# Two transformer layers on one core: VectorE's share of the softmax exponentials, with a cubic or a quadratic polynomial

## The chip, the cores and the metric

The kernel runs on one core of a Trainium2 chip. The metric is the device time of one execution in microseconds, the median of the runs shown. The engines named below are TensorE (PE in the profile, with PEld for its weight loads), VectorE (DVE), ScalarE (ACT), GpSimd (POOL) and SyncE (SP, which issues the DMAs). Each runs its own instructions in program order and waits for the others through semaphores.

## What is computed

Two rounds of attention and a squared-ReLU MLP over 2,048 tokens of width 448, with 16 heads of width 28. All inputs are bf16.

```python
def _A_ref(x, wqkv, wo):
    B, S, D = x.shape
    H = 16; Dh = D // H
    qkv = (lambda x, *d: x.transpose(*d))((x @ wqkv).reshape(B, S, 3, H, Dh), 2, 0, 3, 1, 4)
    q, k, v = qkv[0], qkv[1], qkv[2]
    scale = Dh ** -0.5
    scores = jnp.einsum("bhqd,bhkd->bhqk", q, k) * scale
    p = _softmax(scores, axis=-1)
    o = jnp.einsum("bhqk,bhkd->bhqd", p, v)
    return (lambda x, *d: x.transpose(*d))(o, 0, 2, 1, 3).reshape(B, S, D) @ wo
def _B_ref(x, w1, b1, w2, b2):
    h = jnp.einsum("bsd,df->bsf", x, w1) + b1
    zero = jnp.zeros_like(h)
    r = jnp.where(h > zero, h, zero)
    h = r * r
    out = jnp.einsum("bsf,fd->bsd", h, w2) + b2
    return out
x = A_x
x = x + _A_ref(_layernorm(x, axis=-1), A_wqkv, A_wo)
x = x + _B_ref(_layernorm(x, axis=-1), B_w1, B_b1, B_w2, B_b2)
x = x + _A_ref(_layernorm(x, axis=-1), A_wqkv, A_wo)
x = x + _B_ref(_layernorm(x, axis=-1), B_w1, B_b1, B_w2, B_b2)
```

For each of the two layers, each of the 16 heads has 2,048 x 2,048 scores, and each score needs one exponential. No maximum is subtracted; the sum of the exponentials comes out of the product with V, which carries a column of ones.

## The kernel before

**Score banks.** The scores are cut into units of 128 keys by 512 columns, one PSUM bank each: four heads of a group are done side by side on TensorE (32 rows of the array each), with 256 queries and two key tiles in a unit (128 queries and four key tiles in the last two blocks of layer 1). There are 2,048 such units, or banks. `s_stream` (L818) writes them three at a time into a tile `sc` of three banks (L882); two such tiles alternate (`R_sc`).

**Who takes the exponential.** `e_stream` (L898) has ScalarE turn a whole `sc` tile into a bf16 tile `pt` with one ACTIVATE of Exp (L907), three banks wide, or two banks wide when VectorE takes the third. VectorE's way is `a_unit` and `a_rest` (L954 to L1008). The score arrives scaled by log2(e) times 2^17, so that after adding a bias and limiting it from below (`take`, L965, which writes an int32), the upper 16 bits count half octaves and the lower 16 bits are the place within the half octave. `power` (L981) builds a float of 2 to the half octave from the upper bits; `first` (L988) multiplies it by (f + root), where f is the lower half; `square` (L993) forms (f + lin) * f; `close` (L1003) adds `low` and multiplies with the result of `first`, and writes bf16 into a buffer `pd`. That is five VectorE instructions for a bank. They work in one of two sets of scratch buffers (`R_v`): the tiles v_i, v_e and v_h, or a part of `K_sb` that is not in use at the time. In the second set the result of `square` overwrites the score.

**Who decides.** The kernel text does not fix the order of the work. A planner (`Planner`, L143) runs while the program is built: it holds a clock for each engine, an estimated duration for each piece of work (the second argument of `Op`), and streams with priorities, and it always issues next the piece that can start first by its clocks. `apart` (L774) is asked at each `sc` tile whether VectorE takes the third bank. It says no, among other things, when the scratch sets are taken, when VectorE was occupied over a limit in the last 8 us of the planner's clock (`BUSY`, L797), or when the work that VectorE still owes, `left[0]`, passes `TB` or `TB2` (L799). `left[0]` grows by 2.74 for each bank taken (L970), and falls as its instructions are issued. So the number of banks that go to VectorE is a result of the planner, and durations written in the `Op`s change the order of everything.

**What else the engines do.** TensorE multiplies the exponentials with V (`p_stream`, L1065), and fills in between with projections, w_o, w1 and w2 (`mm_tile`, L606). VectorE empties those banks, does layer norms, the normalisation and the MLP's squared ReLU (L1261, L1268). When the planner sees TensorE little occupied, it repeats score matmuls (`again`, L875) or inserts matmuls whose result nobody reads (`heat`, L1319). While scores are left, ScalarE does nothing but Exp; after the last one (`s_left` empty) it also takes ReLUs and squares (`engs_now`, L440). The last two 128-token blocks of layer 1 go through w_o, layer norm and MLP in the tail (`chain`, L1204).

Of the kernel before, what the change touches and what calls it, by code (L numbers as in the profile page):

```python
# [11 lines left out]
DT = mybir.dt  # L12
AF = mybir.ActivationFunctionType
ALU = mybir.AluOpType
# [9 lines left out]


FRAC = 17
EXP_BIAS = -0.19498194355419685 * 2.0 ** FRAC
EXP_LOW = -56.0 * 2.0 ** FRAC
EXP_BASE = 72.0 * 2.0 ** 23 + 13573.0 * 2.0 ** 7
EXP_POLY = (4.12317870205982 * 2.0 ** 16, 3.06764719893404 * 2.0 ** 16, 29.439149859494734 * 2.0 ** 32)  # L30
OVER = 0.08
QUICK = 2
QUICK3 = 2
# [203 lines left out]
def kernel(  # L237
# [12 lines left out]
    nc = tc.nc  # L250
# [35 lines left out]
    R_v = (Res(1), Res(1))  # L286
# [477 lines left out]
    left = [0.0]  # L764

    def sets_of(unit):

        pi, kb, r, hh = unit
        l, qb, *_ = passes[pi]
        if l == 0:  # L770
            return R_v if 2 <= qb <= 6 else R_v[:1]
        return R_v
# [45 lines left out]
    def s_stream():  # L818
        while at[0] < len(units):
# [5 lines left out]
            def fn(e, gi=gi, us=us, js=js):  # L825
# [17 lines left out]
                if j is None:  # L843
                    next_at(js[-1] + 1)
                else:
                    if not own:
                        us, ks = us[:2], ks[:2]
                        gbuf[gi]["n"] = 2
                    us, ks = us + [units[j]], ks + [3]
                    taken.add(j)  # L850
                    held[0] += 1
                    pending[0] += 1
                    next_at(at[0])
                    if own:
                        x = gbuf[gi]["x"] = Op("PE", 0.0, None)
                        x.res = min((r for r in R_m if r.when() is not None), key=lambda r: r.when())
                        x.turn = len(x.res.rel)
                        x.res.rel.append(None)
                        dst.append(bank(x, "mt"))
                    else:  # L860
                        x = gbuf[gi]["x"] = o
                        o.need = 2
                    pl.spawn(C_PRIO, a_unit(gi, x, dst[-1], us[-1], passes[us[0][0]][0]))
# [28 lines left out]
    def apart_from(gi, t):  # L892

        if "read" in gbuf[gi]:
            tc.declare_no_dep(t.ins, gbuf[gi]["read"].ins, reason="both read the scores, in banks of their own")
        gbuf[gi]["read"] = t
# [21 lines left out]
    def pd_free(unit):  # L918

        pi, kb, r, hh = unit  # L920
        l, qb, *_ = passes[pi]
        if l == 0:
            return (R_pd[0], *(R_pd[1:5] if qb <= 6 else R_pd[3:5]))
        if len(norm_done.get((0, len(blocks[0]) - 1), ())) < G:
            return tuple(R_pd[:1])
        return tuple(R_pd[:1] + R_pd[6:]) if hidden_left[0] else tuple(R_pd[:1] + R_pd[5:])

    def pd_of(o):
        i = R_pd.index(o.res)
        if i == 0:  # L930
            return vp.tile([P, 512], DT.bfloat16, name="pd")[:, :]
        if i < 5:
            return V_sb[1][:, 11 + i, :, :].rearrange("p h r -> p (h r)")
        if i > 5:
            return V_sb[0][:, 8 + i, :, :].rearrange("p h r -> p (h r)")
        return hp.tile([P, QB], DT.bfloat16, name="h")[:, :]
# [5 lines left out]
    def set_of(res, l):  # L942

        k = R_v.index(res)
        two = lambda a: a.rearrange("p (a n) -> p a n", a=2)
        if k == 0:
            i, e, h = two(v_i[:, :]), two(v_e[:, :]), two(v_h[:, :])
        else:
            keys = K_sb[1 - l][:, :, S - 512:S] if l == 0 else K_sb[0][:, :, 0:512]
            i, e = keys[:, 0:2, :].bitcast(DT.int32), keys[:, 2:4, :].bitcast(DT.int32)  # L950
            h = i.bitcast(DT.float32)
        return i, e, h, two

    def a_unit(gi, x, src, unit, l):  # L954
        yield Op("-", 0.0, None, deps=[("s", gi)])
        box = {}

        def take(e):
            pending[0] -= 1
            box["i"], box["e"], box["h"], two = set_of(c.res, l)  # L960
            box["two"] = two
            halves = box["i"].bitcast(DT.uint16).rearrange("p a (n t) -> p a n t", t=2)
            box["f"] = halves[:, :, :, 0]
            box["n"] = box["i"].bitcast(DT.int16).rearrange("p a (n t) -> p a n t", t=2)[:, :, :, 1]
            t = nc.vector.tensor_scalar(out=box["i"], in0=two(src), scalar1=EXP_BIAS,  # L965
                                        scalar2=EXP_LOW, op0=ALU.add, op1=ALU.max)
            if x is gbuf[gi]["s"]:
                apart_from(gi, t)
        c = Op("DVE", 0.69, take, deps=[("s", gi)], acq=sets_of(unit), rel=x)
        left[0] += 2.74  # L970
        yield c
        left[0] -= 0.6
        pl.spawn(lambda now: V_LAST if e_now[1] - gi >= V_AGE or at[0] > ends_at[unit[0]] + V_PAST else V_LATE if now > c.end + V_WAIT else V_PRIO if gi > FIRST else V_FIRST, a_rest(gi, c, box, unit))

    def a_rest(gi, c, box, unit):

        root, lin, low = EXP_POLY
        flt = lambda k: box[k].bitcast(DT.float32)

        def power(e):  # L980
            nc.vector.tensor_scalar(out=box["e"], in0=box["n"], scalar1=2.0 ** 22, scalar2=EXP_BASE,  # L981
                                    op0=ALU.mult, op1=ALU.add)
        p = Op("DVE", 0.42, power, deps=[c])
        yield p
        left[0] -= 0.34

        def first(e):
            nc.vector.scalar_tensor_tensor(out=flt("e"), in0=box["f"], scalar=root, in1=flt("e"),  # L988
                                           op0=ALU.add, op1=ALU.mult)
        g = Op("DVE", 0.684, first, deps=[p])  # L990

        def square(e):
            nc.vector.scalar_tensor_tensor(out=box["h"], in0=box["f"], scalar=lin, in1=box["f"],  # L993
                                           op0=ALU.add, op1=ALU.mult)
        alone = c.res is R_v[0]
        h = Op("DVE", 0.684, square, deps=[c] if alone else [c, g])
        for k in (h, g) if alone else (g, h):
            yield k
            left[0] -= 0.6

        def close(e):
            pd = gbuf[gi]["pd"] = pd_of(o)
            nc.vector.scalar_tensor_tensor(out=box["two"](pd), in0=box["h"], scalar=low, in1=flt("e"),  # L1003
                                           op0=ALU.add, op1=ALU.mult)
        o = Op("DVE", 0.683, close, deps=[g, h], acq=lambda: pd_free(unit), rel=c, sets=("x", gi))
        gbuf[gi]["x"] = o
        yield o
        left[0] -= 0.6  # L1008
# [361 lines left out]
```

## Time and profile before

| what | value |
|---|---|
| median of 3 runs | 875.69 us (875.18 to 875.69) |
| span of the profiled execution, first to last instruction | 872.5 us |
| PE busy | 825.1 us (95%) |
| DVE busy | 822.3 us (94%) |
| ACT busy | 857.0 us (98%) |
| POOL busy | 44.8 us (5%) |
| DMA traffic | 17.98 MB, mean 21 GB/s |

The profiled execution is one run; its span leaves out what lies before the first and after the last instruction, and it is 3.2 us below the median of the timed runs. Busy time of an engine is the union of its instructions; two instructions of one engine can overlap by the latency of the first, so that mean durations times counts come out above the busy time. The mean duration of an ACTIVATE or of a VectorE instruction is therefore longer than the distance from its start to the start of the next.

### The profile page before, as it was taken

Reading aid. Unit: us, or ns where it says so; the run is one execution under the profiler, and the core shown is the slowest. Engines: PE = TensorE matmul, PEld = TensorE weight load, DVE = VectorE, ACT = ScalarE, POOL = GpSimd, SP = SyncE. Lnnn points to the kernel's source line nnn. Section 1 sums busy time; section 2 is a strip of 40 time slices with the busy share of each in tenths; the row PEclk is TensorE's granted clock in tenths of the full one; section 3 lists DMA queues with packets and bytes.
Section 4 is the critical chain, followed back from the end, with each engine's and each line's share of the span. In section 5 each row is a group of like instructions: output and inputs, shape, how many; then the busy total and the mean of one; then the engine's idle time right before and its main releaser. Section 6 shows DMA issues by size and latency. Waiting matters only on the chain.

```text
span 872.5 us, 28714 instructions
## 1 busy us (share of the span) xinstructions
PE 825.1 (95%) x12595; PEld 441.7 (51%) x12595; DVE 822.3 (94%) x1677; ACT 857.0 (98%) x701; POOL 44.8 (5%) x95
## 2 busy tenths in 40 slices
PE   8999999999999999999999999999999999999998
PEld 4455544554545545454454444445454454545556
DVE  7999899999999999999989999999999999999944
ACT  8999999999999999999999999999999999999995
POOL 3100000002000000000000000000000000000000
PEclk9999999999999999999999999999999999999999
DMA  9100100000000000000000000011000000000000
GB/s 251 57 3 2 28 15 15 14 15 16 11 5 15 14 15 14 6 11 14 2 2 3 2 2 2 15 28 28 20 20 25 20 20 26 12 15 15 20 8 17
DMA packets 32313, 17.98 MB, mean 21 GB/s; under 512 B 17786, under 2 KB 31739, under 8 KB 32188
## 3 DMA queue, kind: packets, MB, share of 16 engines
q1 hardware_dynamic: 32188, 16.16, 6.7%
q8 instruction: 98, 1.61, 0.8%
q14 instruction: 27, 0.22, 0.1%
HBM read 13.87 MB, written 2.06 MB: 18 GB/s over the span
## 4 chain that ended last, share of the span: by engine, by line
ACT 46%; DVE 30%; PE 12%; issue 9%; DMA 2%; POOL 1%; SPq 0%; DVEq 0%
ACT pt L907 46%; PE mt L606 6%; PE sc L882 3%; DVE r L1261 3%; DVE V_sb L1003 2%; DVE K_sb L965 2%; DVE v_i L965 2%; DVE K_sb L988 2%; DVE K_sb L993 2%; DVE v_e L988 2%; DVE v_h L993 2%; PE oT L1065 1%; DVE x_sb L1201 1%; DVE st L460 1%; DVE K_sb L981 1%
## 5 line engine op out<-in xcount | busy, mean ns | idle before, releaser
L907 ACT ACTIVATE pt<-sc 128x1536 bf16<-128x1536 f32 (+1 forms) x683 | 845.1, 1481 | 2.7 <-PE sc L882 2.5
L882 PE MATMUL sc<-Q_sb,K_sb 32*128 32x256 bf16 (+1 forms) x5588 | 314.3, 266 | 34.6 <-ACT pt L907 29.0
L882 PEld LDWEIGHTS <-K_sb 32*128 32x128 bf16 x5588 | 140.7, 92 | 214.9 <-issue 177.3
L1065 PE MATMUL oT<-pt,V_sb 128*32 128x256 bf16 (+1 forms) x3998 | 154.4, 268 | 0.3 <-DVE Q_sb L625 0.2
L606 PE MATMUL mt<-xnT,w 128*128 128x256 bf16 (+1 forms) x904 | 119.4, 270 | 0.7 <-DVE oTn L1150 0.2
L1065 PEld LDWEIGHTS <-V_sb 128*32 128x32 bf16 x4352 | 91.0, 96 | 49.8 <-issue 46.7
L606 PEld LDWEIGHTS <-w 128*128 128x128 bf16 x952 | 78.5, 98 | 36.3 <-issue 27.9
L1261 DVE TENSOR_SCALAR r<-mt 128x512 bf16<-128x512 f32 x108 | 73.2, 678 | 4.8 <-PE mt L606 4.5
L965 DVE TENSOR_SCALAR v_i<-sc 128x512 int32<-128x512 f32 x97 | 66.1, 682 | 3.5 <-PE sc L882 3.1
L606 PE MATMUL mt<-w,V_sb 128*128 128x448 bf16 x274 | 67.3, 355 | 0.0
L993 DVE SCALAR_TENSOR_TENSOR v_h<-v_i 128x512 f32<-128x512 uint16 x97 | 65.9, 680 | 0.0
L988 DVE SCALAR_TENSOR_TENSOR v_e<-v_i,v_e 128x512 f32<-128x512 uint16 x97 | 65.7, 677 | 0.0
L1319 PE MATMUL mt<-xn,ident 128*128 128x448 bf16 x171 | 58.3, 357 | 1.1 <-DVE r L1261 0.2
L487 POOL TENSOR_TENSOR ve<-mv,eps_t 128x2 f32<-128x2 f32 (+1 forms) x34 | 13.0, 383 | 813.8 <-DVE mv L465 813.8
L965 DVE TENSOR_SCALAR K_sb<-sc 128x512 int32<-128x512 f32 x75 | 51.2, 683 | 3.1 <-PE sc L882 2.7
L993 DVE SCALAR_TENSOR_TENSOR K_sb<-K_sb 128x512 f32<-128x512 uint16 x75 | 51.0, 681 | 0.7
L988 DVE SCALAR_TENSOR_TENSOR K_sb<-K_sb 128x512 f32<-128x512 uint16 x75 | 51.1, 681 | 0.6
L1201 DVE TENSOR_TENSOR x_sb<-x_sb,mt 128x448 bf16<-128x448 bf16 x61 | 37.3, 611 | 9.8 <-PE mt L606 9.7
L1003 DVE SCALAR_TENSOR_TENSOR V_sb<-v_h,v_e 128x512 bf16<-128x512 f32 x63 | 42.8, 680 | 0.4
L981 DVE TENSOR_SCALAR v_e<-v_i 128x512 int32<-128x512 int16 x97 | 40.1, 414 | 0.3
L460 DVE BATCH_NORM_STATS2 st<-x_sb 128x6 f32<-128x448 bf16 x62 | 38.0, 613 | 0.8 <-DMA x_sb<-in_A_x_dram 0.7
L606 PEld LDWEIGHTS <-V_sb 128*128 128x128 bf16 x302 | 25.0, 98 | 25.1 <-issue 10.1
(105 smaller groups left out, 796.6 us busy)
## 6 DMA issues: line engine op xcount, KB each, us to landing
rec<-scr SPq DMA_DIRECT2D x54, 128.0 KB
x_sb<-in_A_x_dram SPq DMA_DIRECT2D x8, 224.0 KB
out_dram<-x_sb SPq DMA_DIRECT2D x15, 112.0 KB
w<-in_B_w_dram SPq DMA_DIRECT2D x1, 1568.0 KB
w<-in_B_w_dram SPq DMA_DIRECT2D x1, 1344.0 KB
dn<-oT_sb SPq DMA_DIRECT2D x54, 4.0 KB
V_sb<-in_A_wqkv_dram SPq DMA_DIRECT2D x4, 168.0 KB
scr<-dn SPq DMA_DIRECT2D x27, 8.0 KB
```

What stands on the lines that cost most here:

```text
L460: nc.vector.bn_stats(out=box["st"][:, :], in_=x_sb[:, t0 + j, :] if src is None else src())
L606: nc.tensor.matmul(box["t"][:, c0:c0 + n], lhsT=lhsT() if callable(lhsT) else lhsT, rhs=rhs, start=a, stop=b)
L882: nc.tensor.matmul(dst[k][:, i * nt * P:(i + 1) * nt * P], lhsT=K_sb[l][rows, g, (kb + i) * P:(kb + i + 1) * P], rhs=Q_sb[rows, g, t0 * P: ...
L907: t = nc.scalar.activation(out=pt[:, 0:n], in_=gbuf[gi]["sc"][:, 0:n], func=AF.Exp, scale=float(np.log(2.0)) * 2.0 ** -FRAC)
L965: t = nc.vector.tensor_scalar(out=box["i"], in0=two(src), scalar1=EXP_BIAS, scalar2=EXP_LOW, op0=ALU.add, op1=ALU.max)
L981: nc.vector.tensor_scalar(out=box["e"], in0=box["n"], scalar1=2.0 ** 22, scalar2=EXP_BASE, op0=ALU.mult, op1=ALU.add)
L988: nc.vector.scalar_tensor_tensor(out=flt("e"), in0=box["f"], scalar=root, in1=flt("e"), op0=ALU.add, op1=ALU.mult)
L993: nc.vector.scalar_tensor_tensor(out=box["h"], in0=box["f"], scalar=lin, in1=box["f"], op0=ALU.add, op1=ALU.mult)
L1003: nc.vector.scalar_tensor_tensor(out=box["two"](pd), in0=box["h"], scalar=low, in1=flt("e"), op0=ALU.add, op1=ALU.mult)
L1065: nc.tensor.matmul(box["t"][DHP * hh:DHP * hh + DHP, 0:n], lhsT=V_sb[l][:, kb + i, 4 * g + hh, :], rhs=p[:, c0:c0 + n], start=begin and kb ...
L1261: nc.vector.tensor_scalar(out=r[:, 0:w], in0=t[:, 0:w], scalar1=0.0, scalar2=None, op0=ALU.max)
L1319: nc.tensor.matmul(t[:, 0:D], lhsT=ident[:, :], rhs=xns[0][:, 0:D], start=True, stop=True)
```

## The change

VectorE's polynomial on the half octave becomes a quadratic: `first` is gone, `close` multiplies with the result of `power` directly, and the constants are those of the quadratic. Four VectorE instructions are left for a bank: `take`, `power`, `square`, `close`. In the second scratch set `square` now follows `power`. The planner's count of owed work goes from 2.74 to 2.14 for each bank. Nothing else is edited; the order of the instructions is planned anew.

```diff
 FRAC = 17
-EXP_BIAS = -0.19498194355419685 * 2.0 ** FRAC
+EXP_BIAS = -0.08179355555318127 * 2.0 ** FRAC
 EXP_LOW = -56.0 * 2.0 ** FRAC
-EXP_BASE = 72.0 * 2.0 ** 23 + 13573.0 * 2.0 ** 7
-EXP_POLY = (4.12317870205982 * 2.0 ** 16, 3.06764719893404 * 2.0 ** 16, 29.439149859494734 * 2.0 ** 32)
+EXP_BASE = 91.0 * 2.0 ** 23 + 13573.0 * 2.0 ** 7
+EXP_POLY = (4.803267716767392 * 2.0 ** 16, 14.031064225079138 * 2.0 ** 32)
...
         c = Op("DVE", 0.69, take, deps=[("s", gi)], acq=sets_of(unit), rel=x)
-        left[0] += 2.74
+        left[0] += 2.14
         yield c
...
-        root, lin, low = EXP_POLY
-        flt = lambda k: box[k].bitcast(DT.float32)
+        lin, low = EXP_POLY
...
-        def first(e):
-            nc.vector.scalar_tensor_tensor(out=flt("e"), in0=box["f"], scalar=root, in1=flt("e"),
-                                           op0=ALU.add, op1=ALU.mult)
-        g = Op("DVE", 0.684, first, deps=[p])
-
         def square(e):
             nc.vector.scalar_tensor_tensor(out=box["h"], in0=box["f"], scalar=lin, in1=box["f"],
                                            op0=ALU.add, op1=ALU.mult)
-        alone = c.res is R_v[0]
-        h = Op("DVE", 0.684, square, deps=[c] if alone else [c, g])
-        for k in (h, g) if alone else (g, h):
-            yield k
-            left[0] -= 0.6
+        h = Op("DVE", 0.684, square, deps=[c] if c.res is R_v[0] else [c, p])
+        yield h
+        left[0] -= 0.6
 
         def close(e):
             pd = gbuf[gi]["pd"] = pd_of(o)
-            nc.vector.scalar_tensor_tensor(out=box["two"](pd), in0=box["h"], scalar=low, in1=flt("e"),
+            nc.vector.scalar_tensor_tensor(out=box["two"](pd), in0=box["h"], scalar=low, in1=box["e"].bitcast(DT.float32),
                                            op0=ALU.add, op1=ALU.mult)
-        o = Op("DVE", 0.683, close, deps=[g, h], acq=lambda: pd_free(unit), rel=c, sets=("x", gi))
+        o = Op("DVE", 0.683, close, deps=[p, h], acq=lambda: pd_free(unit), rel=c, sets=("x", gi))
```

## The prediction

> **What bounds the kernel now.** I read the page's engine totals first, then ScalarE's groups by shape, then who waits for whom, then the chain of waits in a steady stretch.
>
> ```profile
> span 872.5 us, 28714 instructions
> PE 825.1 (95%) x12595; PEld 441.7 (51%) x12595; DVE 822.3 (94%) x1677; ACT 857.0 (98%) x701; POOL 44.8 (5%) x95
> PEclk9999999999999999999999999999999999999999
> ```
>
> Three engines are nearly full, so shares alone do not decide. The groups of ScalarE by shape, and the waits of ScalarE and TensorE on each other, do:
>
> ```profile
> L907 ACT ACTIVATE pt<-sc 128x1536 bf16<-128x1536 f32 x510 | 726.6, 1589 | 2.7 <-PE sc L882 2.5
> L907 ACT ACTIVATE pt<-sc 128x1024 bf16<-128x1024 f32 x173 | 199.0, 1163 | 0.0
> L907 ACT ACTIVATE pt<-sc x683: 1017/1552/1757, 10.7 to 856.5; 128x1536 bf16<-128x1536 f32 x137, 128x1024 bf16<-128x1024 f32 x34
> ACT pt L907 <- PE sc L882: 2.5, 6, 0.7
> PE sc L882 <- ACT pt L907: 29.0, 87, 0.6
> ```
>
> From 10.7 us until its last Exp (start 856.5, end about 857.9) ScalarE waited for scores only 6 times, 2.5 us together. TensorE waited 87 times, 29.0 us, for ScalarE to free a score tile. ScalarE sets the pace of 847 of the 872.5 us. The chain in a steady stretch shows its step:
>
> ```profile
> 702.98 1.27 ACT pt L907
> 704.31 1.25 ACT pt L907
> 705.64 1.22 ACT pt L907
> 706.97 1.20 ACT pt L907
> 708.30 1.17 ACT pt L907
> 709.63 0.75 ACT pt L907
> 710.54 1.16 ACT pt L907
> ```
>
> Starts lie 1.33 us apart for a three-bank Exp, and 0.91 after the one at 709.63, a two-bank one. So a bank is worth 0.42 to 0.43 us of ScalarE's time; the mean durations above say the same (1.589 - 1.163 = 0.426). Check: 510 x 1.33 + 173 x 0.91 = 836 us of the 847; the remaining 11 us are under 0.02 us for each Exp.
>
> VectorE is behind nothing for long: it is idle a few per cent and nobody on the path waits for it much. What it does for the path is take banks: 172 of 2,048 (97 + 75, below).
>
> **The change, part by part.** First what VectorE pays for a bank:
>
> ```profile
> L965 DVE TENSOR_SCALAR v_i<-sc 128x512 int32<-128x512 f32 x97 | 66.1, 682 | 3.5 <-PE sc L882 3.1
> L988 DVE SCALAR_TENSOR_TENSOR v_e<-v_i,v_e 128x512 f32<-128x512 uint16 x97 | 65.7, 677 | 0.0
> L965 DVE TENSOR_SCALAR K_sb<-sc 128x512 int32<-128x512 f32 x75 | 51.2, 683 | 3.1 <-PE sc L882 2.7
> L988 DVE SCALAR_TENSOR_TENSOR K_sb<-K_sb 128x512 f32<-128x512 uint16 x75 | 51.1, 681 | 0.6
> 562.10 0.68 DVE L965 TENSOR_SCALAR v_i<-sc 128x512 int32<-128x512 f32 x1
> 562.71 0.68 DVE L993 SCALAR_TENSOR_TENSOR K_sb<-K_sb 128x512 f32<-128x512 uint16 x1
> 563.30 0.42 DVE L981 TENSOR_SCALAR v_e<-v_i 128x512 int32<-128x512 int16 x1
> 563.64 0.68 DVE L1003 SCALAR_TENSOR_TENSOR pd<-K_sb 128x512 bf16<-128x512 f32 x1
> 564.26 0.42 DVE L1093 TENSOR_TENSOR oT_sb<-oT,K_sb 128x256 f32<-128x256 f32 x1
> ```
>
> Instructions of 0.68 us start 0.60 apart, the `power` of 0.42 takes a step of 0.34. *Removed:* `first`, 172 x 0.60 = 103 us of VectorE. By itself that would be worth nothing: no row shows ScalarE waiting for VectorE. It is worth something only if more banks move. *Added:* they do. In the instruction lists of the two built programs the three-bank Exps go from 510 to 475, the two-bank ones from 173 to 208 (683 in all, as before), and the `take`s from 172 to 207 (117 + 90). 35 banks leave ScalarE: 35 x 0.426 = **14.9 us less on the path**. They cost VectorE 35 x (3 x 0.60 + 0.34) = 75 us, so VectorE ends 28 us lower, near 794, or 92% of the new span: it has room to take them. The four operations left have the same shapes and types as before, so their durations stand; `square` now follows `power` where it used to follow `first`, and `close` follows `square` in both sets, a dependence between neighbours that the second set already has today.
>
> Can TensorE keep up? Its necessary work is unchanged; the planner's fillers shrink. In the lists the repeated score matmuls fall by 156 (192 fewer of 256 columns, 36 more of 128), the matmuls that nobody reads rise from 171 to 176.
>
> ```profile
> L882 PE MATMUL sc<-Q_sb,K_sb 32*128 32x256 bf16 x5052 | 296.7, 271 | 32.0 <-ACT pt L907 27.0 <-DVE K_sb L965 0.5 <-DVE h L1268 0.2
> L882 PE MATMUL sc<-Q_sb,K_sb 32*128 32x128 bf16 x536 | 17.6, 216 | 2.6 <-ACT pt L907 2.0 <-DVE v_e L988 0.2
> L1319 PE MATMUL mt<-xn,ident 128*128 128x448 bf16 x171 | 58.3, 357 | 1.1 <-DVE r L1261 0.2 <-DVE xnT L522 0.2
> ```
>
> Busy time by count: 192 x 0.059 - 36 x 0.033 - 5 x 0.34 = 8.4 us less. That is less than the 14.9 us by which the scoring gets shorter, so TensorE's wait for ScalarE should fall from 29 us to about 22. It stays a wait of TensorE, so ScalarE stays the bound. Is the fit equally good everywhere? I added up each engine's steps along its list, and asked how far it falls behind ScalarE's running sum between one point and a later one. VectorE falls behind by up to 2.3 us among the first twenty `take`s (0.6 before) and by 0.8 later (1.0 before). TensorE falls behind by up to 3.1 us between the 50th and the 100th Exp (1.2 before) and about as before from the 150th on. A `take` that is late holds its score tile, TensorE then waits to refill it, and ScalarE waits for TensorE:
>
> ```profile
> PEld L882 <- DVE K_sb L965: 5.8, 15, 0.8
> PEld L882 <- DVE v_i L965: 3.1, 10, 0.4
> ```
>
> Today those are 8.9 us of TensorE's waits, of which 2.5 at most reach ScalarE. The after side has no row. Bounds for new idle time of ScalarE: -2.5 us (every present wait gone) and +4.2 (the extra lags of 1.7 and 1.9, and 0.6 for 25 more places in which two two-bank Exps are neighbours: 36 against 11). I take **+1.0**, nearer to the lower end, since today's lag of about 1 us already lets only 2.5 us through in 847.
>
> **The tail** is moved by the new order. After the last Exp the old list has 14 w2 matmuls of 448 columns and 90 w1 matmuls of 128; the new one has 29 and 96. The second-to-last block's MLP is later: none of its w2 product is done when the last scores end, and its 15 matmuls (one is the bias) now stand at the very end, behind the last block's.
>
> ```profile
> 857.98 0.41 PE L1065 MATMUL oT<-pt,V_sb 128*32 128x128 bf16 x16
> 858.52 1.06 PE L606 MATMUL sc<-xnT,w 128*128 128x128 bf16 x16
> 860.24 2.62 PE L606 MATMUL mt<-w,V_sb 128*128 128x448 bf16 x13
> 863.60 1.95 PE L606 MATMUL sc<-xnT,w 128*128 128x128 bf16 x32 [0.33 <-DVE xnT L522]
> 866.86 2.06 PE L606 MATMUL sc<-w,V_sb 128*128 128x320 bf16 x14
> 868.81 0.94 PE L606 MATMUL sc<-w,V_sb 128*128 128x128 bf16 x14
> 869.80 0.29 DVE L1201 TENSOR_TENSOR x_sb<-x_sb,sc 128x128 bf16<-128x128 bf16 x1 [0.35 <-PE sc L606]
> L1201 DVE TENSOR_TENSOR x_sb<-x_sb,mt 128x448 bf16<-128x448 bf16 x61 | 37.3, 611 | 9.8 <-PE mt L606 9.7
> 860.00:872.50 12.50, 9.43 (x108) 7.15 (x106) 5.25 (x13) 3.32 (x7) 0.75 (x2) 1.00 0.06 20
> ```
>
> The tail after the last Exp lasts 872.5 - 857.9 = 14.6 us, and TensorE has hardly a gap in it until 869.75: today's w2 matmuls already fill the layer norm's wait. So more matmuls lengthen it. One of 448 columns steps 0.19 us ((2.62 - 0.35) / 12), one of 128 about 0.06 (1.95 / 32). Added: 15 x 0.19 + 6 x 0.06 = 3.2, and the last addition into x is one of 448 columns (0.61) instead of 128 (0.29): 0.3. A rest comes from the order: the last block's w1 starts behind 16 of the other block's, some 0.5 us later than its input is ready. Bounds: +0.3 (the matmuls find gaps, only the longer addition remains) and +5 (1 us more, the length of the 16 matmuls at 858.52, if the last store's larger piece or another chunk also lies in line). I take **+3.9**, near the sum, since the gaps are gone already.
>
> **Sum.** On the profiled execution: 872.5 - 14.9 + 1.0 + 3.9 = 862.5. The median of the runs lies 3.2 above that span (875.7 against 872.5), so **865.7 us**.
>
> One rule speaks against the change. The Trainium skill, "Perfetto Trace Analysis", section "Identifying the Most-Contended Engine", says to take the engine with the highest occupancy as the bottleneck and work on that one first; here that is ScalarE, and the edit shortens VectorE's work. By that rule alone the sum would be 875.7, no change. The row of 683 Exps agrees with the rule about who is the bottleneck, but the banks are handed from one engine to the other, so the edit does reach ScalarE. The same section calls matmul busy time a poor measure of TensorE's headroom and wants the weight loads' share looked at: here 51% beside 95%, which agrees with TensorE being the one that waits and lowers the chance of the third rival.
>
> **Rivals.** *The tail gives nothing back* (the new w2 matmuls fall into waits of the layer norm, +0.3): 872.5 - 14.9 + 1.0 + 0.3 + 3.2 = 862.1. Against it: TensorE's 11.8 us after the last Exp are almost gapless.
>
> *The opening starves* ScalarE by the full lags on VectorE and TensorE, and the tail takes its upper bound: +4.2 and +5, 870.0. For it: the sums above; against it: lag is not idle time as long as two score tiles are in hand.
>
> *ScalarE waits at each shorter Exp, and the kernel gets slower.* Where ScalarE works for only 0.91 us on a tile, TensorE must have the other refilled in that time, after VectorE has read its third bank. If each of the 35 additional two-bank Exps cost the longest single wait in the waits above, 0.7 us: 35 x 0.7 = 24.5, and 865.7 - 1.0 + 24.5 = 889. From 11 us, or 0.31 us for each, the gain is eaten. Against it: today 173 of them come with 2.5 us of waits in all, 0.014 each.
>
> *The time does not change*: the freed VectorE time stays idle, or ScalarE's time does not follow the number of banks. 875.7. Against it: the list moves 35 banks, and the two shapes differ by 0.426 us.
>
> **Chances.** Forecast (863.5 to 868) 62%; no cost in the tail 14%; starved opening (868 to 873) 15%; no change 4%; slower 5%. Without the last two and the outermost of the third, the range is 861.5 to 871.5. A measurement of this kernel can tell about 0.2%, 1.8 us, from no change. Faster by more: 62 + 14 + 15 = 91%; same 4%; slower 5%.
>
> **What would show it.** Exps of 1536 and 1024 columns 475 and 208 with means still near 1.59 and 1.16, and ScalarE's last Exp ending near 844 instead of 857.9: the bank term right. Waits of L907 for scores under 5 us: the idle term right; over 11 us, the slower rival. VectorE near 794 us busy. From the last Exp to the end 18.5 us instead of 14.6, with 15 matmuls of 448 columns as the last on TensorE: the tail term. A tail of 15 us would make the sum too long by 3.6; a granted clock below full, or Exps whose mean duration rose, would break the pricing itself.

## The result and the profile after

The changed kernel takes 863.88 us (median of 4 runs, 863.83 to 864.58) where the kernel before takes 875.43 beside it: a ratio of 0.9866, 95% interval 0.9852 to 0.988. Run again, beside the kernel before, it gave 864.15 against 873.27, ratio 0.9886 (0.9866 to 0.9906). The forecast was 865.7.

The page's totals of the changed kernel, its two shapes of Exp on ScalarE (count, busy us, mean ns, idle before and what ended it), and the row of all 683 Exps (shortest, median and longest ns, start of the first and of the last):

```profile
span 862.1 us, 28421 instructions
PE 817.5 (95%) x12444; PEld 439.2 (51%) x12444; DVE 797.1 (92%) x1644; ACT 842.1 (98%) x702; POOL 42.8 (5%) x95
L907 ACT ACTIVATE pt<-sc 128x1536 bf16<-128x1536 f32 x475 | 686.3, 1618 | 1.4 <-PE sc L882 1.4
L907 ACT ACTIVATE pt<-sc 128x1024 bf16<-128x1024 f32 x208 | 238.9, 1196 | 2.6 <-PE sc L882 2.6
L907 ACT ACTIVATE pt<-sc x683: 1018/1565/1839, 10.4 to 842.0; 128x1536 bf16<-128x1536 f32 x115, 128x1024 bf16<-128x1024 f32 x56
```

ScalarE is as full as before (98%), VectorE less so (92% for 94%), and the counts are 475 and 208. Who waits for whom, from the same kernel's list of waits (us in total, times, longest):

```profile
ACT pt L907 <- PE sc L882: 4.0, 4, 2.6
PE sc L882 <- ACT pt L907: 26.2, 80, 0.7
```

TensorE still waits for ScalarE 6.5 times as long as the reverse. ScalarE's waits rose from 2.5 to 4.0 us, and 2.6 of that is one wait. The timeline around it (start, length, what; the bracket is the idle time before):

```profile
79.46 0.40 PE L1057 MATMUL oT<-pt,V_sb 128*32 128x256 bf16 x6 [0.88 <-ACT pt L907]
79.79 1.05 PE L606 MATMUL mt<-xnT,wk 128*128 128x256 bf16 x8
80.67 0.92 PE L606 MATMUL mt<-wv,xnT 128*128 128x448 bf16 x4
80.87 0.69 DVE L629 CAST K_sb<-mt 128x512 bf16<-128x512 f32 x1 [0.42 <-PE mt L606]
81.52 0.61 PE L882 MATMUL sc<-Q_sb,K_sb 32*128 32x256 bf16 x12
82.02 2.37 ACT L907 ACTIVATE pt<-sc 128x1024 bf16<-128x1024 f32 x2 [2.62 <-PE sc L882]
```

The planner put the next two tiles of scores (the 55th and 56th) behind keys that are only now projected (wk) and cast into `K_sb`; it is the fifteenth of the sixteen casts of layer 0's keys. In TensorE's order the projection stands behind a product with V, and there TensorE first waited 0.88 us for an Exp. In the kernel before, the 55th tile stands behind the same cast:

```profile
77.04 0.69 DVE L629 CAST K_sb<-mt 128x512 bf16<-128x512 f32 x1 [0.62 <-PE mt L606]
```

There ScalarE starts its 55th Exp at 80.4; in the changed kernel it is free for it at 79.4. So ScalarE comes to these keys 1.0 us sooner, and the keys come 3.8 us later (77.04 to 80.87). The later keys are the larger part.

The tail, from the timeline of the changed kernel; the first row is the last five Exps, the others are the rows that answer to those shown before:

```profile
836.72 6.74 ACT L907 ACTIVATE pt<-sc 128x1536 bf16<-128x1536 f32 x5
843.58 0.41 PE L1057 MATMUL oT<-pt,V_sb 128*32 128x128 bf16 x16
847.15 1.06 PE L606 MATMUL sc<-xnT,w 128*128 128x128 bf16 x16
849.49 1.95 PE L606 MATMUL sc<-xnT,w 128*128 128x128 bf16 x32
855.79 2.81 PE L606 MATMUL sc<-w,V_sb 128*128 128x448 bf16 x14
858.64 0.62 DVE L1193 TENSOR_TENSOR x_sb<-x_sb,sc 128x448 bf16<-128x448 bf16 x1 [2.55 <-PE sc L606]
```

The last Exp ends at 836.72 + 6.74 = 843.5 (857.9 before) and the kernel 18.6 us later (14.7 before). The 14 matmuls of 448 columns and the long addition stand at the end, and TensorE has no gap ahead of them.

So the difference of the spans, 872.5 - 862.1 = 10.4, is made up of 14.1 less between the first and the last Exp (847.2 to 833.1), 0.3 less ahead of the first Exp (10.7 to 10.4), and 4.0 more behind the last.

### The profile page after: what moved, and what is told of

Same layout as the page of the kernel before. It is cut to its first block, busy times and chain, and to the rows that moved or that the text cites. A ratio compares the mean times of both kernels' runs of the same rounds, so it can differ in the third digit from the quotient of the medians.

```text
span 862.1 us, 28421 instructions
## 1 busy us (share of the span) xinstructions
PE 817.5 (95%) x12444; PEld 439.2 (51%) x12444; DVE 797.1 (92%) x1644; ACT 842.1 (98%) x702; POOL 42.8 (5%) x95
## 4 chain that ended last, share of the span: by engine, by line
ACT 68%; PE 12%; issue 11%; DVE 6%; DMA 1%; POOL 0%; SPq 0%; ACTq 0%; DVEq 0%
ACT pt L907 68%; PE mt L606 5%; PE sc L882 3%; PE oT L1057 2%; PE sc L606 1%; PE mt L1311 1%; DVE r L1253 1%; DVE K_sb L965 1%; DVE st L460 1%; DMA rec<-scr 1%; DVE K_sb L987 0%; DVE V_sb L995 0%; DVE v_i L965 0%; DMA scr<-dn 0%; DMA V_sb<-in_A_wqkv_dram 0%
## 5 line engine op out<-in xcount | busy, mean ns | idle before, releaser
L907 ACT ACTIVATE pt<-sc 128x1536 bf16<-128x1536 f32 (+1 forms) x683 | 829.6, 1490 | 4.1 <-PE sc L882 4.0
L882 PE MATMUL sc<-Q_sb,K_sb 32*128 32x256 bf16 (+1 forms) x5432 | 307.8, 265 | 32.6 <-ACT pt L907 26.2
L606 PEld LDWEIGHTS <-w 128*128 128x128 bf16 x952 | 78.0, 98 | 37.7 <-issue 29.2
L965 DVE TENSOR_SCALAR v_i<-sc 128x512 int32<-128x512 f32 x117 | 80.1, 685 | 6.5 <-PE sc L882 5.9
L987 DVE SCALAR_TENSOR_TENSOR v_h<-v_i 128x512 f32<-128x512 uint16 x117 | 79.9, 683 | 0.0
L965 DVE TENSOR_SCALAR K_sb<-sc 128x512 int32<-128x512 f32 x90 | 61.7, 686 | 5.4 <-PE sc L882 4.6
L606 PE MATMUL mt<-w,V_sb 128*128 128x448 bf16 (+1 forms) x274 | 66.3, 348 | 0.0
L987 DVE SCALAR_TENSOR_TENSOR K_sb<-K_sb 128x512 f32<-128x512 uint16 x90 | 61.7, 685 | 1.0 <-PE mt L606 0.2
L980 DVE TENSOR_SCALAR v_e<-v_i 128x512 int32<-128x512 int16 x117 | 49.1, 419 | 0.6
L1193 DVE TENSOR_TENSOR x_sb<-x_sb,mt 128x448 bf16<-128x448 bf16 (+1 forms) x61 | 37.0, 611 | 7.0 <-PE mt L606 6.9
L1057 PE MATMUL oT<-V_sb,V_sb 128*32 128x256 bf16 x238 | 42.5, 276 | 0.0
L980 DVE TENSOR_SCALAR K_sb<-K_sb 128x512 int32<-128x512 int16 x90 | 37.9, 421 | 0.5
```

Of the source, the lines that this page charges most:

```text
L606: nc.tensor.matmul(box["t"][:, c0:c0 + n], lhsT=lhsT() if callable(lhsT) else lhsT, rhs=rhs, start=a, stop=b)
L882: nc.tensor.matmul(dst[k][:, i * nt * P:(i + 1) * nt * P], lhsT=K_sb[l][rows, g, (kb + i) * P:(kb + i + 1) * P], rhs=Q_sb[rows, g, t0 * P: ...
L907: t = nc.scalar.activation(out=pt[:, 0:n], in_=gbuf[gi]["sc"][:, 0:n], func=AF.Exp, scale=float(np.log(2.0)) * 2.0 ** -FRAC)
L1057: nc.tensor.matmul(box["t"][DHP * hh:DHP * hh + DHP, 0:n], lhsT=V_sb[l][:, kb + i, 4 * g + hh, :], rhs=p[:, c0:c0 + n], start=begin and kb ...
L1193: nc.vector.tensor_tensor(out=x_sb[:, tb, lo:hi], in0=x_sb[:, tb, lo:hi], in1=t[:, 0:hi - lo], op=ALU.add)
```

## The experiments

**The operation removed, no bank moved.** The edit on the kernel before, with the quadratic's constants put in:

```diff
         def first(e):
-            nc.vector.scalar_tensor_tensor(out=flt("e"), in0=box["f"], scalar=root, in1=flt("e"),
-                                           op0=ALU.add, op1=ALU.mult)
+            pass
         g = Op("DVE", 0.684, first, deps=[p])
```

The planner still counts the operation, so every other instruction stays where it was.

> The order of before is kept to the last instruction and only the 172 multiplications by (f + root) on VectorE are gone (with the quadratic's constants); no bank moves. Theory (the time follows the banks that ScalarE keeps, and VectorE's freed time is worth nothing by itself): 510 and 173 Exps as before, VectorE about 103 us less busy, time within 0.2% of before, 874 to 876. Rival (VectorE's lateness was on the path too, so the shorter polynomial pays by itself): up to the 2.5 us of ScalarE's waits and 9 us of TensorE's waits for VectorE go, 865 to 873.

Measured: 871.63 us against 873.68, ratio 0.9979 (0.997 to 0.9987). The page's totals and the two waits that moved:

```profile
span 870.0 us, 28556 instructions
PE 824.1 (95%) x12595; PEld 442.8 (51%) x12595; DVE 735.6 (85%) x1505; ACT 856.0 (98%) x701; POOL 41.9 (5%) x95
ACT pt L907 <- PE sc L882: 1.0, 2, 0.6
DVE v_i L965 <- PE sc L882: 29.2, 44, 2.4
```

VectorE's busy time fell by 87 us (103 expected) and the kernel's time by 2. The 871.63 alone would lie among the rival's 865 to 873, but on this chip the kernel before took 873.68, so the ratio decides. The freed time is idle: VectorE now waits 29.2 us for scores at `take` in the v_i set alone (3.1 before). ScalarE's own waits fell from 2.5 to 1.0 us. So the theory holds for most of it, but not to the last 0.2%: a fast VectorE is worth some 2 us by itself. The waits that ScalarE no longer has are 1.5 of them. The rest of the change's gain needs the banks.

**The banks moved, the operation kept.** The edit on the changed kernel, with the cubic's constants:

```diff
             nc.vector.tensor_scalar(out=box["e"], in0=box["n"], scalar1=2.0 ** 22, scalar2=EXP_BASE,
                                     op0=ALU.mult, op1=ALU.add)
+            nc.vector.scalar_tensor_tensor(out=box["e"].bitcast(DT.float32), in0=box["f"], scalar=root, in1=box["e"].bitcast(DT.float32),
+                                           op0=ALU.add, op1=ALU.mult)
```

> The order of after (207 banks on VectorE) with the cubic's fifth operation put back right behind the power, unknown to the planner. Theory (VectorE has to pay for the banks that it takes; without the saved operation it becomes the bound): VectorE's steps between its first and last bank go from 727 us, where ScalarE has 761, to 727 + 207 x 0.60 = 851, so the time rises by about 90 us, to 940 to 960, and ScalarE waits for scores by that much. Rival (VectorE is off the path, the banks alone count): 864 to 870.

Measured: 1007.4 us against 873.68, ratio 1.1532 (1.1503 to 1.1561). The totals, ScalarE's waits, and three rows of VectorE's timeline:

```profile
span 1003.5 us, 28603 instructions
PE 850.7 (85%) x12444; PEld 436.4 (43%) x12444; DVE 935.6 (93%) x1851; ACT 868.6 (87%) x702; POOL 41.6 (4%) x95
ACT pt L907 <- PE sc L882: 115.2, 173, 3.4
507.35 0.42 DVE L980 TENSOR_SCALAR v_e<-v_i 128x512 int32<-128x512 int16 x1
507.80 0.69 DVE L982 SCALAR_TENSOR_TENSOR v_e<-v_i,v_e 128x512 f32<-128x512 uint16 x1
508.41 0.68 DVE L965 TENSOR_SCALAR K_sb<-sc 128x512 int32<-128x512 f32 x1
```

The direction is the theory's, the size is not: 141 us over the changed kernel's span, not 90. Two things were left out. VectorE's busy time rises by 138.5 us, and its idle time does not shrink (1003.5 - 935.6 = 67.9 us; 862.1 - 797.1 = 65.0 in the changed kernel): the 34 us of slack that I had counted on were not to be had. And the added operation reads what the one just before it writes: it starts 0.45 after `power` (507.35 to 507.80) instead of 0.34 to 0.35. TensorE's granted clock was 0.974 in this run, but TensorE was only 85% busy. In this order the 35 banks cannot be had without the operation that is saved; whether another order could fit some of them with five operations, no run shows.

**The matmuls at the end left out.** The edit on the changed kernel; of the second-to-last block's w2 product only the bias is left, so its MLP output is not computed:

```diff
                 for c0, n, lhsT, rhs, a, b, _ in part:
+                    if cut and not a:
+                        continue
                     nc.tensor.matmul(box["t"][:, c0:c0 + n], lhsT=lhsT() if callable(lhsT) else lhsT, rhs=rhs,
-                                     start=a, stop=b)
+                                     start=a, stop=b or cut)
...
-                    add_to_x(tb, lo, hi), 0.15 + (hi - lo) / 950, [*([] if own_deps else [hacts[-1][2]]), ("w2",), ("b2",)],
+                    add_to_x(tb, lo, hi), 0.15 + (hi - lo) / 950, [*([] if own_deps else [hacts[-1][2]]), ("w2",), ("b2",)], cut=(l, qb) == (1, len(blocks[1]) - 2),
```

> Order of after; of the second-to-last block of layer 1 the 14 w2 matmuls that stand last on TensorE are left out (the bias matmul and the addition stay). Theory (TensorE is the bound of the tail, each of them is 0.19 us of it): 14 x 0.19 = 2.7 us less, 861.2, and the tail after the last Exp 16.0 instead of 18.6 us. Rival (the stores or the last block's own chain end the kernel): no change, 863.9.

Measured: 860.93 us, ratio 0.9861 (0.9846 to 0.9876). Its span, its last Exps and its last addition into x:

```profile
span 858.9 us, 28393 instructions
837.49 5.41 ACT L909 ACTIVATE pt<-sc 128x1536 bf16<-128x1536 f32 x4
855.45 0.61 DVE L1195 TENSOR_TENSOR x_sb<-x_sb,sc 128x448 bf16<-128x448 bf16 x1
```

The tail is 858.9 - 842.9 = 16.0 us, as expected; the last addition starts at 855.45 instead of 858.64. These matmuls set the end of the kernel. The ratio is no guide here: the kernel before took 873.68 on this chip and 875.43 beside the first run of the changed kernel, whose second run, beside a kernel before of 873.27, gave 0.9886.

**The changed kernel again**, beside the next three on one chip:

> The changed kernel again, for comparison with the next three on the same chip. All theories: 0.9866 of before, as measured (0.9852 to 0.988).

Measured: 864.15 us, ratio 0.9886; ScalarE's waits for scores 3.9 us, the longest again 2.6.

**VectorE's first bank later.** One constant of the changed kernel:

```diff
-LEAD = 15
+LEAD = 30
```

> The changed kernel with LEAD 30 instead of 15: VectorE takes no bank before the 30th score tile (8 two-bank Exps among the first 60 instead of 12), 476 and 207 Exps in all. Theory (the single wait of 2.6 us of ScalarE near 79 us comes from ScalarE reaching the keys before their projection is done, because it has fewer banks to do in the opening): that wait is gone, one bank more on ScalarE costs 0.4, so 2.2 us less than the changed kernel on the same chip. Rival (the wait belongs to VectorE's late reading of a score bank or to the load on TensorE, wherever ScalarE is): the wait stays or shows up later, no change within 0.5 us.

Measured: 862.15 us, ratio 0.9863 (0.9844 to 0.9881), 2.0 us under the changed kernel on the same chip. The two intervals overlap, and the two profiled spans are only 0.7 apart (861.6 and 860.9), so the size is less certain than the place. The waits show the place:

```profile
ACT pt L907 <- PE sc L882: 2.0, 4, 0.8
```

The wait of 2.6 us is gone and none of that length came up elsewhere, with one bank less on VectorE. So the wait belongs to the opening. But the constant also gave a new order, and the fifteenth cast of the keys starts much earlier in it:

```profile
76.70 0.68 DVE L629 CAST K_sb<-mt 128x512 bf16<-128x512 f32 x1
```

That is 4.2 us before the changed kernel's, while ScalarE begins its 55th Exp at 80.8, 1.4 us after it is free for it in the changed kernel. So the theory, ScalarE reaching the keys too early, names the smaller of two shifts, and this run does not separate them. Up to 79.4 us VectorE takes ten banks in the changed kernel, eight in the kernel before and seven here; that this is what delays the keys is not shown.

**The second-to-last block's normalisation.** One constant of the changed kernel:

```diff
-QUICK = 2
+QUICK = 1
```

> The changed kernel with QUICK 1 instead of 2: three instead of two head groups of the second-to-last block of layer 1 are normalised on VectorE by transposes instead of through three DMAs, so that the block's MLP stands before the end of the scores; banks as in the changed kernel (475 and 208). Theory (the 3.9 us lost in the tail are the other block's matmuls behind the last Exp): the tail after the last Exp falls from 18.6 to 14.6 us or a little less, as in before, and the time by about 4 us. Rival (the tail is long because the scores end earlier, and the work shows up before the last Exp as idle time of ScalarE): the last Exp ends some 4 us later, no change.

This kernel does something else than its expectation says. The head groups that are not normalised on VectorE go in pairs; with three of four on VectorE the fourth has no partner, its pair never completes, and the block's w_o, layer norm and MLP are left out altogether. So it shows what the tail is without any of that block's work. Measured: 861.13 us, ratio 0.9857 (0.9835 to 0.988). Its windows at the end (PE, weight loads, DVE, ACT and POOL busy us with counts; then the granted clock) and three rows of its timeline:

```profile
842.00:846.00 4.00, 0.98 (x30) 0.36 (x18) 2.23 (x7) 0.68 (x1) 0.19 (x1) 0.93 0.01 4
846.00:850.00 4.00, 2.41 (x22) 2.25 (x23) 1.01 (x3) 0.00 (x0) 0.56 (x1) 0.50 0.00 0
850.00:854.00 4.00, 4.00 (x47) 3.81 (x46) 1.40 (x4) 1.79 (x3) 0.00 (x0) 0.71 0.00 0
854.00:858.90 4.90, 2.29 (x26) 1.73 (x24) 1.19 (x4) 0.00 (x0) 0.00 (x0) 1.00 0.08 23
847.07 0.61 PE L510 MATMUL sc<-ident,xn 128*128 128x128 bf16 x4 [2.28 <-DVE xn L570]
848.20 1.87 PE L606 MATMUL sc<-xnT,w 128*128 128x128 bf16 x16 [0.52 <-DVE xnT L522]
849.86 3.11 PE L606 MATMUL mt<-xnT,w 128*128 128x128 bf16 x32
```

With the whole block's work away the tail still takes 858.9 - 842.7 = 16.2 us, more than the kernel before needs with that work in it (14.7). While the last block goes through its layer norm, TensorE has nothing to do for 2.28 us and little before it, the granted clock falls to 0.50, and the last block's 16 w1 matmuls take 1.87 us instead of 1.06. The clock is back at full by 854. The Trainium skill, "TensorE: Matmul & The Clock Gate", section "What's actually happening", says that TensorE's clock drops to half after an idle window of about 3.4 us and comes back after a busy one of that length; the rows agree with the half, and windows of 4 us do not show the lengths. So the other block's matmuls in the tail were not only load: in the changed kernel, which has them, the granted clock is 1.00 in each window of 4 us from 843 to 855.

**Both constants.**

> The changed kernel with LEAD 30 and QUICK 1. Theory (the two losses are independent): both gains add up, 2.2 + 4 = 6.2 us less than the changed kernel on the same chip, near 0.979 to 0.980 of before. Rival (one of them returns as a wait in another place): not more than the larger of the two alone, 4 us.

It leaves the same block out. Measured: 859.75 us, ratio 0.9838 (0.9819 to 0.9856), 4.4 us under the changed kernel. With that block missing, this tells nothing of the tail of a whole kernel; it shows only that the opening's 1.4 us (861.13 - 859.75) come on top of another tail.

**The planner's constants set anew for the quadratic.** The edit changes 24 constants of the changed kernel, among them:

```diff
-QUICK = 2
+QUICK = 4
...
-L0E = 1310
-L0N = 7.6
+L0E = 1370
+L0N = 7.2
...
-LEAD = 15
+LEAD = 20
...
-MORE = 3
-HEAT = 0.76
+MORE = 2
+HEAT = 0.6
```

> The quadratic with 23 of the planner's constants set anew for it (two-bank Exps 211, three-bank 472; VectorE takes no bank before the 20th tile; after the last score 20 matmuls of 448 columns on TensorE instead of 36). Theory (the quadratic's loss of 1.5 us by one wait in the opening and 4 us in the tail is a matter of the order, not of the polynomial): 3 banks more are worth 1.3 us, the tail comes back to 15 to 16 us, the opening's wait is gone: 857 to 859 where the changed kernel has 864. Rival (fewer fillers lower the granted clock, or the waits return elsewhere): 862 or more.

Measured: 859.07 us against 875.38, ratio 0.9807 (0.9793 to 0.9822). That is under both kernels, and its interval does not overlap the changed kernel's two. Its totals, ScalarE's waits and its last Exps:

```profile
span 857.7 us, 28640 instructions
PE 798.8 (93%) x12543; PEld 436.1 (51%) x12543; DVE 802.3 (94%) x1653; ACT 841.4 (98%) x701; POOL 44.5 (5%) x95
ACT pt L907 <- PE sc L882: 2.9, 6, 0.6
838.50 4.02 ACT L907 ACTIVATE pt<-sc 128x1536 bf16<-128x1536 f32 x3
```

The tail is 857.7 - 842.5 = 15.2 us, with all of the work in it; the longest wait of ScalarE is 0.6. Most of the gain over the changed kernel, 3.4 of the 4.4 us between the two spans, is the tail: its last Exp ends only 1 us earlier. A second set, with QUICK left at 2 and MORE at 1, did the same:

> The same idea with another set of constants (also 472 and 211, tail with 20 matmuls of 448 columns and fewer of 128 behind the last Exp, fewer repeated score matmuls: MORE 1). Theory: 857 to 859. Rival: as above, 862 or more.

Measured: 859.34 us, ratio 0.9814 (0.9796 to 0.9832). And that second set on the kernel before:

> The kernel before (cubic, five operations) with the constants of e7_tuned_b: 510 and 173 Exps, as before. Theory (the constants alone pay next to nothing, what pays is the banks that the quadratic lets VectorE take): within 3 us of before. Rival (the constants carry the gain): 5 us or more under before.

Measured: 875.6 us, ratio 1.0003 (0.9993 to 1.0013): this set alone pays nothing. With the quadratic, which had left a long tail, it pays. The first set was not run on the kernel before.

## Why the prediction was right

**The banks.** 35 banks at 0.426 us were put at 14.9. The counts came out as forecast. The time between the first and the last Exp fell by 14.1, with 1.5 us more of waits in it; without those it is 15.6, a little more than the term. The step that the price rests on held: the two shapes differ by 1618 - 1196 = 422 ns after. One of the prediction's signs misled: it said that Exps with a longer mean would break the pricing. The means did rise, by 29 and 33 ns, and the price held, since the step from one Exp to the next did not follow the mean (last section).

**The freed time of VectorE.** The prediction said that it is worth nothing by itself. The kernel with the old order and without the operation is 2 us faster, so this step was too strong. In the sum it is hidden: by ScalarE's waits, the shorter polynomial took 1.5 us away (2.5 to 1.0, order kept) and the new order added 3.0 (1.0 to 4.0). VectorE's load came out at 797.1 us (794 forecast), with some luck: taking the operation out freed 87 us instead of 103, and the 35 banks then added 61.5 (735.6 to 797.1) instead of 75. TensorE's wait for ScalarE came out at 26.2 (22 forecast).

**New idle time.** +1.0 was taken, +1.5 measured. The running sums had shown TensorE behind between the 50th and the 100th Exp, and the one long wait lies there, ahead of the 55th. The reason given, a late `take` that holds its tile, is not what the rows show there: the scores waited for keys that the new order projects later.

**The tail.** +3.9 was taken, +4.0 measured, and the kernel without the last 14 matmuls gave back what they were priced at. The rival of a tail without cost is out. So is the starved opening, which had both terms at their upper bounds, +4.2 and +5.

**The rivals.** The slower one needed 0.31 us for each additional two-bank Exp; all waits at two-bank Exps are 2.6 us, in one of 208. The rule of the Trainium skill, "Perfetto Trace Analysis", section "Identifying the Most-Contended Engine", to work on the engine with the highest occupancy first, was right on which engine it is (ACT, 98%), but the edit reaches that engine. That it does so only by moving banks was shown from both sides, by the order kept (2 us) and by the operation kept (141 us slower).

**From the span to the time.** The mis-sized term is the 3.2 us between the profiled span and the median. Wherever a run's time and span are both on record, they lie 1.7 to 1.9 apart (863.88 and 862.1 for the profiled run of the changed kernel). By that, the profiled run of the kernel before took about 874.3, and the other 1.4 us of the 3.2 are the difference of that run from the median. With 1.8 the forecast would have been 864.3. The span itself came out at 862.1, against 862.5 in the sum, and part of that closeness is luck: 0.7 more from the banks and 0.3 less ahead of the first Exp, which the sum did not have, stand against 0.5 more waits and 0.1 more tail.

## What to carry to other kernels

Where a planner shares one kind of work between engines, an edit that makes one engine's share cheaper is worth the share that moves, priced at the engine that sets the pace (here 0.43 us of ScalarE a bank), and next to nothing if none moves. Count the instructions in the two lists before pricing anything. When the main loop gets shorter, look at its two ends: work that used to hide in it comes out behind it (4.0 us here, most of which another order took back), and the new order may bring inputs of the opening later than the main loop wants them (here the keys, 3.8 us).

## What was not expected of the hardware

Neighbours on VectorE cost more when the second reads what the first writes. From the changed kernel's timeline:

```profile
44.17 0.43 DVE L980 TENSOR_SCALAR v_e<-v_i 128x512 int32<-128x512 int16 x1
44.52 0.69 DVE L987 SCALAR_TENSOR_TENSOR v_h<-v_i 128x512 f32<-128x512 uint16 x1
45.12 0.42 DVE L1085 TENSOR_TENSOR K_sb<-oT,K_sb 128x256 f32<-128x256 f32 x1
49.12 0.69 DVE L987 SCALAR_TENSOR_TENSOR v_h<-v_i 128x512 f32<-128x512 uint16 x1
49.85 0.69 DVE L995 SCALAR_TENSOR_TENSOR V_sb<-v_h,v_e 128x512 bf16<-128x512 f32 x1
50.46 0.68 DVE L629 CAST K_sb<-mt 128x512 bf16<-128x512 f32 x1
```

`square` (L987) is followed after 0.60 us by an instruction that has nothing to do with it (44.52 to 45.12), though it lasts 0.69; `close`, which reads its result, starts 0.73 after it (49.12 to 49.85). The 0.13 us between are the price of the dependence between these neighbours. Between `power` and the operation put back behind it, it was about 0.1 (0.45 instead of 0.35, 44.17 to 44.52). What in the engine makes the difference, the rows do not show. The Trainium skill, "VectorE: DVE Perf Modes", section "Terms", entry DRAIN, read by itself, has the next operation wait after every one until the pipe is empty; in these rows only the dependent neighbour starts after its predecessor's end.

The mean duration of a three-bank Exp moved between kernels without the pace moving with it. In the kernel with the old order and without the operation the groups by shape and the row of all Exps read:

```profile
L907 ACT ACTIVATE pt<-sc 128x1536 bf16<-128x1536 f32 x510 | 731.4, 1621 | 1.1 <-PE sc L882 1.0
L907 ACT ACTIVATE pt<-sc x683: 1017/1591/1757, 10.6 to 854.0; 128x1536 bf16<-128x1536 f32 x137, 128x1024 bf16<-128x1024 f32 x34
```

The mean is 1621 ns against 1589 before, 32 ns more for each, and yet the same 683 Exps went by in 2.4 us less (start of the first to start of the last: 843.4 against 845.8). The duration is not the step by which ScalarE goes on; only the difference of the two shapes was safe to use.
